# Linear attention with a rational FFN on one core: the hand-ordered instruction table is replaced by another one, and the last three slices share buffers

## The chip, the cores and the metric

One NeuronCore of a Trainium2 chip runs the whole program. The metric is device time in microseconds (us) of one execution. Five engines work from queues of their own: TensorE (PE, with its weight loads shown as PEld), VectorE (DVE), ScalarE (ACT), GpSimd (POOL) and SyncE (SP), which here issues the DMAs. An engine runs its queue strictly in order, and an instruction that needs another engine's result waits at the head of its queue.

## The reference

The inputs are r, k, v (4 batches, 8 heads, 768 steps, 48 wide), the decay w and the bonus u per head and channel, the two FFN weights w_in (384 x 2048) and w_out (2048 x 384), and the coefficients a (4) and b (2). The first stage is a recurrence over time:

```python
for t in range(S):
    cur = einsum('bhd,bhe->bhde', u * k[t], v[t])
    y[t] = einsum('bhd,bhde->bhe', r[t], state + cur)
    state = w * state + einsum('bhd,bhe->bhde', k[t], v[t])
```

Its output, as 3072 rows of 384, goes through an FFN whose activation is a ratio of a cubic and a quadratic:

```python
h = x @ w_in
P = a[0] + a[1]*h + a[2]*h**2 + a[3]*h**3
Q = 1 + |b[0]|*|h| + |b[1]|*h**2
out = (P / (Q + 1e-6)) @ w_out
```

## The kernel before, in words

**Attention.** Time is cut into 24 blocks of 128 rows (6 in each of 4 batches; block n is batch n % 4). For each block r and k are loaded (`Lr`, `Lk`) and multiplied with tables of powers of w (`sr`, `sk`), transposed on PE (`tr`, `tk`) and copied out of PSUM by ACT (`tre`, `tke`); PE makes the scores (`a`), DVE masks them (`ae`), PE makes the state's update (`kv`), which `kve` adds to the state, `ca` carries the state to the next block, PE makes the output (`y`). The bonus term is four multiplications and a sum on the side (`ba`, `bb`, `bs`, `bv`), and `ye` adds it. `x` transposes the block's output, and `xh`, `xl` split it into a high and a low part.

**FFN.** Two blocks make a tile of 256 rows (12 tiles). The 2048 hidden columns of a tile are 16 pieces j of 128; four of them make a slice (`SL`, line 36), and the last four pieces of the last tile are three slices of 2, 1 and 1: slices 47, 48 and 49 of 0 to 49. A slice s goes: `f1` on PE, nine matmuls per piece, into one of two PSUM buffers (h0, h1); three stages on ACT (`z`, `q`, and `t`), `u3` on DVE, `ln` and `ex` on ACT, then `hi`, `p`, `d`, `lo` on DVE; `f2` on PE, twelve matmuls for each of two halves; after a tile's last slice `os` takes the result out of PSUM and `od` stores it. `f1` of slice s+2 needs the buffer of slice s, so it waits for `lo` of slice s.

**Weights.** The 28 weight pieces come as 8-byte floats and are turned into pairs of 4-byte parts: `cl` loads one, ACT (`c0`, `cu`, `ch`), DVE (`c2`, `c3`) and POOL (`cr`, `co`) convert it.

**Which DVE work has all its inputs in SBUF.** The multiplications `sr`, `sk`, `ba`, `bb`, `bv` (lines 500 to 522), `ca` (line 611), the copy `LV` on DVE, `co` on DVE, and of the slice work only `p` (line 700, `q = (q + QE) * hi`). The other DVE work reads at least one operand from PSUM.

**Order.** Nothing here is scheduled by the compiler. `ORDER` (line 49) is a string of some 1,800 tasks, written by a search outside this file. A task is a name with its numbers, a letter for its engine (P, D, A, G for POOL, S for SP) and, where it takes a buffer, the buffer's name: `p.12D`, `hi.12Dta3`, `f1.12.0Ph0`. The program runs through the string once and issues each task to its engine, so the string fixes every engine's queue, which engine does a movable task, and which buffer is reused when. `warm.N` puts N small bf16 matmuls (line 797) without use into PE's queue, ahead of a task that follows them in the queue.

**End.** Line 371 and lines 374 and 375 (`flagt`, `flagm`) reduce a check on the inputs to one number, which all engines read at the end to skip a general path for odd inputs.

Of the kernel before, what the change touches and what calls it, by code (L numbers as in the profile page):

```python
# [49 lines left out]
pad.1G coefS plG mskG st0.0G st0.1G idG pad.0G wS Lv.3S betaA uwS ubG warm.54P ubpPpa0 cl_D ctrA st0.2A st0.3A Lv.2S LV.1.1.0A  # L50
LV.1.0.0A Lr.1S sqD Lr.2S pad.2G pow.0D pow.1D warm.10P turn.0.0Ppa1 warm.6P turn.1.0P inv.0D Lr.0S ubeA warm.13P turn.0.1Ppa0
pow.2D LV.1.0.1A Lk.0S Lk.2S warm.4P turn.2.0P tab.0A sr.1G inv.1D inv.2D warm.29P turn.2.1P Lk.1S Lv.0S LV.1.1.1A wlD turn.1.1P
tab.1A cl.2S tr.1Ph0 tre.1.0A tre.1.1A sr.0D wpPpa1 w128A cl.5S sr.2D sk.0D sk.2D ba.2Dm0 tr.0Ppa0 tre.0.1A warm.9P kv.2Ph1 sk.1D
tre.0.0A kve.2.0A bb.2D ba.0Dm1 Lr.3S ba.1Gm2 bs.2D bv.2D Lv.1S tk.0Ph0 tke.0A c0.2A c2.2Dh0 bb.1G kv.0Ppa1 kve.0.1A warm.2P
a.0Ppa0 bb.0G kve.2.1A warm.6P tk.1Ph1 c3.2D cu.2A cr.2Gta0 Lk.3S cl.6S tke.1A warm.16P a.1Ph0 kve.0.0A tk.2Ppa1 ae.0.1D cl.12S
bs.0D c0.5A ch.2A ae.0.0D bv.0G bs.1D LV.0.1.1A cl.1S ae.1.0D Lr.4S c2.5Dh1 LV.0.0.1A LV.0.0.0A ae.1.1D warm.36P kv.1Ph0 cl.4S
sr.3G c3.5D LV.0.1.0A y.0Ppa0 sk.3G ba.3Dm3 co.2D c0.6A bb.3D Lk.5S ca.0.1G cu.6A Lk.4S kve.1.0A c2.6Dh1 tke.2A ye.0D ca.0.0G
kve.1.1A c3.6D cr.6Gta1 c0.12A c2.12Dh0 c3.12D bv.1D warm.7P tr.2Ppa1 warm.2P kv.3Ppa0 c0.1A c2.1Dh1 c3.1D tre.2.0A cu.12A
cr.12Gta2 tre.2.1A bs.3D warm.13P x.0Ph0 cl.26S kve.3.0A kve.3.1A cu.5A warm.11P a.2Ppa1 ae.2.0D sr.4G y.1Ph1 tr.3Ppa0 ch.12A
cl.0S cu.1A sk.5G ae.2.1D ca.1.1G c0.4A warm.5P y.2Ppa1 ye.1D tk.3Ph1 xh.0A sk.4D tre.3.1A ca.1.0D xl.0D warm.3P tr.4Ph0 c0.26A  # L60
Lr.5S tre.3.0A tke.3A cr.5Gta3 ye.2D ba.4Dm1 c0.0A ch.6A warm.2P x.2Ppa0 xh.2A bv.3G c2.26Dh1 c3.26D cu.4A cr.1Gta4 xl.2D a.3Ppa1
warm.2P tk.4Ph1 ae.3.1D tre.4.0A sr.5G cl.20S Lv.5S tre.4.1A warm.21P kv.5Ph0 bb.4G cl.3S cl.9S ch.5A co.5G ae.3.0D c2.0Dpa0 c3.0D
ch.1A co.1G Lv.4S cu.20A tke.4A bs.4D c0.20A cl.10S cu.3A cl.11S kve.5.1D cu.0A cr.0Gta5 c2.4Dpa1 c3.4D cr.4Gta6 warm.16P x.1Ph1
xh.1A c0.3A xl.1D a.4Ppa0 warm.20P kv.4Ph1 cu.9A c2.3Dpa1 c3.3D cl.15S ch.0A co.0G cr.3Gta0 cu.26A cr.26Gta3 cl.14S cl.8S kve.5.0D
kve.4.1D c0.10A c2.10Dh0 c3.10D kve.4.0D warm.3P tk.5Ppa1 tke.5A cu.10A warm.14P y.3Ppa1 ye.3D c0.11A cu.11A ch.3A ba.5Gm0 c0.15A
f1.0.0Ph0 bv.4G LV.2.0.0S c2.11Dpa1 c3.11D cr.11Gta4 cu.15A LV.2.1.1S x.3Ph1 xh.3A ch.26A c0.9A c2.15Dpa1 c0.14A f1.0.1P f1.0.2P
bb.5G co.26G LV.2.1.0S ch.11A xl.3D tr.5Ph1 tre.5.1A tre.5.0A c3.15D co.12G ae.4.1D LV.2.0.1S ae.4.0D Lr.6S c2.14Dpa1 bs.5D
f1.0.3P warm.6P f1.1.0Ph1 cl.24S Lr.7S c3.14D z.0Ata5 c2.20Dpa0 c3.20D t.0Ata3 u3.0D warm.7P a.5Ppa1 ch.4A cu.8A cl.27S warm.1P
y.4Ppa0 cl.7S cl.13S ae.5.0D q.0A ln.0A f1.1.1P co.6G bv.5G cr.15Gta2 ch.15A ye.4D warm.5P x.4Ppa0 xh.4A cr.20Gta1 ch.20A Lk.6S
# [867 lines left out]
```

## Time and profile before

| | us |
|---|---|
| median of 3 runs | 567.09 (566.33 to 570.70) |
| the profiled execution, its own time | 566.86 |
| its span, first to last instruction | 565.1 |
| PE busy | 550.0 |
| DVE busy | 471.7 |
| ACT busy | 397.0 |
| POOL busy | 163.1 |

The span is what the traces count from; the profiled execution's own time is 1.8 us longer, and lies 0.2 us under the median. The mean granted TensorE clock is 0.997 of full speed. A "busy" PE is not PE at its peak: the ends of matmuls are modelled, and one that is 0.28 us long starts every 0.12 us.

### The profile page before, as it was taken

The page shows a single profiled execution, that of the slowest core. Times are in us where ns is not written, and L with a number is a line of the kernel's source. Part 1 is how long each engine was busy: PE and PEld are TensorE (multiplying, and loading weights), DVE is VectorE, ACT ScalarE, POOL GpSimd, SP SyncE. Part 2 cuts the span into 40 slices and gives each one's busy share as a digit, 9 for nine tenths or more (in the row PEclk, how much of TensorE's full clock was granted, in tenths as well). Part 3 has the DMA queues.
Part 4 walks back from the last instruction along what each step waited for, and adds up shares of the span by engine and source line. Part 5 has one row for each costly group of instructions (what it writes and reads, how often), then busy time and mean ns, then how long its engine had stood idle before and what let it go on. Part 6 is the DMA issues. An engine that isn't in the chain of part 4 may idle for free.

```text
span 565.1 us, 13792 instructions
## 1 busy us (share of the span) xinstructions
PE 550.0 (97%) x5916; PEld 527.3 (93%) x5916; DVE 471.7 (83%) x576; ACT 397.0 (70%) x522; POOL 163.1 (29%) x189
## 2 busy tenths in 40 slices
...
DMA packets 95273, 34.69 MB, mean 61 GB/s; under 512 B 88546, under 2 KB 91620, under 8 KB 95204
## 3 DMA queue, kind: packets, MB, share of 16 engines
...
## 4 chain that ended last, share of the span: by engine, by line
PE 71%; DVE 17%; ACT 6%; issue 3%; POOL 1%; DVEq 0%; ACTq 0%; POOLq 0%
PE h L644 26%; PE o L648 8%; PE o L650 8%; PE o L649 8%; PE y L600 4%; DVE q L700 4%; PE a L550 4%; DVE g L696 4%; PE kv L572 4%; DVE h L704 3%; PE idle_bank L797 3%; DVE h L691 3%; ACT z L683 2%; ACT z L687 2%; PE tk L527 2%
## 5 line engine op out<-in xcount | busy, mean ns | idle before, releaser
L644 PE MATMUL h<-xthi,wi 128*128 128x256 f32 x1152 | 218.3, 284 | 2.4 <-DVE l L709 2.1
L644 PEld LDWEIGHTS h<-xthi,wi 128*128 128x128 f32 x1152 | 180.6, 188 | 6.7 <-PE o L650 2.2
L644 PE MATMUL h<-xtlo,wi 128*128 128x256 f32 x576 | 160.8, 279 | 0.0
L648 PE MATMUL o<-wo,g 128*128 128x384 f32 x384 | 132.4, 345 | 0.0
L650 PE MATMUL o<-wo,l 128*128 128x384 f32 x384 | 129.5, 337 | 1.0 <-DVE l L709 1.0
L649 PE MATMUL o<-wo,g 128*128 128x384 f32 x384 | 129.2, 336 | 0.0
L644 PEld LDWEIGHTS h<-xtlo,wi 128*128 128x128 f32 x576 | 108.4, 188 | 0.0
L696 DVE SCALAR_TENSOR_TENSOR g<-h,sig,z 128x1024 fp32r<-128x1024 f32 (+2 forms) x50 | 61.9, 1238 | 47.1 <-ACT z L687 46.4
L679 ACT ACTIVATE z<-h,off,root 128x1024 f32<-128x1024 f32 (+2 forms) x50 | 58.6, 1172 | 42.6 <-PE h L644 34.2
L683 ACT ACTIVATE z<-q,sig 128x1024 f32<-128x1024 f32 (+2 forms) x50 | 56.0, 1119 | 30.6 <-DVE h L691 29.5
L670 ACT ACTIVATE q<-h 128x1024 f32<-128x1024 f32 (+2 forms) x50 | 49.5, 990 | 38.8 <-PE h L644 27.0
L650 PEld LDWEIGHTS o<-wo,l 128*128 128x128 f32 x384 | 72.2, 188 | 1.5 <-DVE l L709 1.5
L648 PEld LDWEIGHTS o<-wo,g 128*128 128x128 f32 x384 | 72.2, 188 | 0.8 <-ACT os L756 0.2
L649 PEld LDWEIGHTS o<-wo,g 128*128 128x128 f32 x384 | 72.3, 188 | 0.0
L691 DVE SCALAR_TENSOR_TENSOR h<-z,sig,h 128x1024 f32<-128x1024 f32 (+2 forms) x50 | 62.0, 1240 | 5.5 <-ACT z L679 3.0
L700 DVE SCALAR_TENSOR_TENSOR q<-q,sig,g 128x1024 f32<-128x1024 f32 (+2 forms) x50 | 64.6, 1292 | 1.9
L704 DVE SCALAR_TENSOR_TENSOR h<-h,sig,q 128x1024 f32<-128x1024 f32 (+2 forms) x50 | 62.5, 1250 | 1.6
L709 DVE TENSOR_TENSOR l<-h,z 128x1024 fp32r<-128x1024 f32 (+2 forms) x50 | 59.1, 1181 | 2.8 <-DVE h L704 0.5
L674 ACT ACTIVATE q<-q,off,root 128x1024 f32<-128x1024 f32 (+2 forms) x50 | 60.6, 1211 | 1.1
L687 ACT ACTIVATE z<-z 128x1024 f32<-128x1024 f32 (+2 forms) x50 | 51.4, 1027 | 1.5
L522 POOL TENSOR_TENSOR m<-vn,dt 128x384 f32<-128x384 f32 x16 | 15.3, 962 | 121.9 <-DVE dt L518 121.9
L508 POOL TENSOR_TENSOR m<-rh,kh 128x384 f32<-128x384 f32 x17 | 17.4, 1028 | 101.0 <-DVE rh L504 48.1
...
## 6 DMA issues: line engine op xcount, KB each, us to landing
...
coef<-in_moe_a_dram SPq DMA_DIRECT2D x1, 2.0 KB, 2.6
```

The lines of the kernel that those rows point to most:

```text
L644: nc.tensor.matmul(o, wi_of(j, cc, part), x_[:, cc], start=(n == 0), stop=(n == 3 * NCC - 1))
L648: nc.tensor.matmul(o, hi, wo_of(j, HI), start=first, stop=False)
L649: nc.tensor.matmul(o, hi, wo_of(j, LO), start=False, stop=False)
L650: nc.tensor.matmul(o, lo, wo_of(j, HI), start=False, stop=last)
L674: nc.scalar.activation(g["q"], g["q"], AF.Square, scale=RB, bias=KB)
L683: nc.scalar.activation(g["z"], g["q"], AF.Ln, bias=QE)
L687: nc.scalar.activation(g["z"], g["z"], AF.Exp, scale=-1.0)
L691: nc.vector.scalar_tensor_tensor(g["h"], g["t"], KAP, g["h"], op0=ALU.add, op1=ALU.mult)
L696: nc.vector.scalar_tensor_tensor(g["hi"], g["h"], c0, g["z"], op0=ALU.add, op1=ALU.mult)
L700: nc.vector.scalar_tensor_tensor(g["q"], g["q"], qe, g["hi"].bitcast(F32), op0=ALU.add, op1=ALU.mult)
L704: nc.vector.scalar_tensor_tensor(g["h"], g["h"], c0, g["q"], op0=ALU.add, op1=ALU.subtract)
L709: nc.vector.tensor_mul(g["lo"], g["h"], g["z"])
```

## The change

The whole of `ORDER` is replaced by another table of the same tasks. The new one comes from a search whose durations for GpSimd and DVE were read from the trace, and whose model lets GpSimd and DVE instructions run at the same time without ever excluding each other. What it moves is read off the two tables:

| | before | after |
|---|---|---|
| matmuls in `warm` groups, all / ahead of `f1.0.0` | 439 / 304 | 380 / 256 |
| DVE tasks with all inputs in SBUF, without the 50 `p` | 53 | 34 |
| of these ahead of `f1.8.0` in the table | 17 | 9 |
| POOL's elementwise tasks, all / ahead of `f1.8.0` | 166 / 95 | 190 / 101 |
| POOL tasks between `hi.s` and `lo.s` in the table, s = 0 to 8 | 13 | 32 |
| the same, s = 9 to 24 / s = 25 to 49 | 12 / 3 | 12 / 2 |
| `cl.6` in SP's queue | after `Lk.3` | after `Lr.0`, ahead of `Lr.2` |

The last tile's end is ordered anew, the last three slices share buffers, and a store may be issued by another engine than SP:

```diff
+f1.46.1P hi.45Dta0 p.45D d.45D flagmD f1.46.2P f1.46.3P z.46Ata2 f2.44.0P t.46Ata5 u3.46D q.46A ln.46A f2.44.1P lo.45Dta4
+f1.47.0Ph1 f1.47.1P ex.46A f2.45.0P f2.45.1P hi.46Dta1 p.46D d.46D lo.46Dta3 f1.48.0Ph0 f1.49.0P z.47Ata6 t.47A u3.47D q.47A
+ln.47A ex.47A hi.47Dta0 z.48Ata4 z.49A t.48A p.47D t.49A u3.48D d.47D u3.49D q.48A lo.47D q.49A ln.48A ex.48A hi.48Dta2 p.48D
+ln.49A ex.49A hi.49D d.48D p.49D lo.48D d.49D lo.49D f2.46.0P f2.46.1P f2.47.0P f2.47.1P f2.48.0P f2.48.1P f2.49.0P f2.49.1P
+os.49.0A od.11.0A os.49.1D od.11.1S
...
     def f1(s, jj):
         f, j0, _ = SL[s]
-        if jj == 0:
+        if s == NS - 1:
+            hps[s] = hps[s - 1][:, GW // 2 : GW]
+        elif jj == 0:
             hps[s] = ps_h.tile([P, GW], F32, tag=here[0], name=f"h{s}")
...
+    packs = {}
+    PACK = {NS - 3: (0, 0), NS - 2: (1, 0), NS - 1: (1, 2 * N1)}
+
     def ew_tile(s, nm, dt=F32):
         n = SL[s][2] * N1 if s in range(NS) else GW
+        if s in PACK:
+            place, at_ = PACK[s]
+            key = place, dt
+            if key not in packs:
+                packs[key] = ew.tile([P, GW], dt, tag=here[0], name=f"{nm}{s}")
+            return packs[key][:, at_ + n * (nm in "zl") : at_ + n * (nm in "zl") + n]
...
-    def put_dma(f, hf):
+    def put_dma(f, hf, e):
         bi, i = blk(2 * f + hf)
-        nc.sync.dma_start(out[ds(bi * S + i * P, P), :], oss.pop((f, hf)))
+        e.dma_start(out[ds(bi * S + i * P, P), :], oss.pop((f, hf)))
```

The order of the old table at the same place was `f1.47.0 f1.47.1 f2.45.0 ... f2.45.1 f1.48.0 f2.46.0 f2.46.1 f1.49.0 flagt flagm f2.47 f2.48 f2.49 os.49.0A od.11.0S os.49.1A od.11.1S`, with each of the last three slices in buffers of its own.

## Rows read from the trace of the kernel before

**Rows 1.** The page, section 1: busy us (share of the span) xinstructions.

```profile
PE 550.0 (97%) x5916; PEld 527.3 (93%) x5916; DVE 471.7 (83%) x576; ACT 397.0 (70%) x522; POOL 163.1 (29%) x189
```

**Rows 2.** Windows by stage, and `f1.45`, then `f2.43`: length, busy us (xinstructions), clock, DMA share, GB/s.

```profile
core 0: us, PE busy (x) PEld busy (x) DVE busy (x) ACT busy (x) POOL busy (x), PEclk, DMA share, GB/s
0.00:47.57 47.57, 44.30 (x866) 40.08 (x866) 40.92 (x88) 41.01 (x90) 32.36 (x51) 1.00 0.96 233
47.57:133.58 86.01, 83.95 (x932) 80.84 (x928) 81.77 (x101) 76.34 (x110) 65.87 (x66) 1.00 0.44 107
...
180.13:530.28 350.15, 348.42 (x3428) 337.03 (x3427) 283.77 (x308) 231.32 (x259) 44.97 (x51) 1.00 0.13 30
...
521.92:526.12 4.20, 4.20 (x38) 4.20 (x38) 1.83 (x2) 2.64 (x3) 0.00 (x0) 1.00 0.00 0
526.12:530.28 4.16, 4.16 (x26) 4.07 (x25) 3.98 (x5) 2.60 (x3) 0.00 (x0) 1.00 0.00 0
...
530.28:565.10 34.82, 26.83 (x170) 24.89 (x169) 20.76 (x27) 18.92 (x27) 0.00 (x0) 0.95 0.09 32
```

**Rows 3.** Waits of PE: who waited for whom, us in total, times, longest.

```profile
PE h L644 <- DVE l L709: 2.1, 4, 1.0
PE x L619 <- DVE m L605: 1.2, 1, 1.2
```

**Rows 4.** Timeline of PE around warm groups: start, length, instruction, [idle before].

```profile
29.65 0.78 PE L797 MATMUL idle_bank<-wones 128*128 128x128 bf16 x11
30.39 0.27 PE L550 MATMUL a<-ysa,kt 64*64 64x64 f32 x1
...
77.72 1.44 PE L797 MATMUL o<-wones 128*128 128x128 bf16 x23 [1.15 <-ACT os L756]
```

**Rows 5.** Timeline of ACT in the prologue: the first power table leaves PSUM.

```profile
10.41 0.48 ACT L348 COPY wrn<-ptab 128x384 f32<-128x384 f32 x1 [0.28 <-PE ptab L345]
```

**Rows 6.** Timelines of POOL and DVE around 62 us.

```profile
61.37 1.02 POOL L504 TENSOR_TENSOR rh<-rh,wrn 128x384 f32<-128x384 f32 x1
62.35 2.97 POOL L420 TENSOR_TENSOR wo<-bwo,wo 128x384 fp32r<-128x384 f32 x2
...
62.28 2.18 DVE L700 SCALAR_TENSOR_TENSOR q<-q,sig,g 128x1024 f32<-128x1024 f32 x1
```

**Rows 7.** Line 700, stretch 0 to 133.58 us: duration ns min/median/max.

```profile
L700 DVE SCALAR_TENSOR_TENSOR q<-q,sig,g x7: 1277/1285/2177, 62.3 to 128.2; 128x1024 f32<-128x1024 f32 x7
```

**Rows 8.** Groups by line: busy us, mean ns; line 700 to 133.58 us, line 500 whole.

```profile
L700 DVE SCALAR_TENSOR_TENSOR q<-q,sig,g 128x1024 f32<-128x1024 f32 x7 | 10.7, 1527 | 0.3
...
L500 DVE TENSOR_TENSOR kh<-kh,wkn 128x384 f32<-128x384 f32 x10 | 6.1, 622 | 0.8 <-DMA kh<-in_k_dram 0.8
```

**Rows 9.** Timelines of DVE, PE and ACT in the last tile, by time.

```profile
538.77 1.22 DVE L709 TENSOR_TENSOR l<-h,z 128x1024 fp32r<-128x1024 f32 x1
540.13 0.36 PE L644 MATMUL h<-xthi,wi 128*128 128x256 f32 x1 [0.98 <-DVE l L709]
545.20 1.23 DVE L709 TENSOR_TENSOR l<-h,z 128x1024 fp32r<-128x1024 f32 x1
548.55 0.75 DVE L696 SCALAR_TENSOR_TENSOR g<-h,sig,z 128x512 fp32r<-128x512 f32 x1 [1.46 <-ACT z L687]
556.60 0.48 DVE L700 SCALAR_TENSOR_TENSOR q<-q,sig,g 128x256 f32<-128x256 f32 x1
557.65 0.42 DVE L709 TENSOR_TENSOR l<-h,z 128x256 fp32r<-128x256 f32 x1
557.99 0.27 DVE L374 TENSOR_REDUCE oks<-flagt 1x1 f32<-1x128 f32 x1
558.29 0.14 DVE L375 CAST okf<-oks 1x1 int32<-1x1 f32 x1
558.61 1.11 ACT L756 ACTIVATE os<-o,sig 128x384 f32<-128x384 f32 x2 [2.63 <-PE o L650]
```

**Rows 10.** Timeline of SP at the end: both last stores.

```profile
559.22 1.66 SPq L764 DMA_DIRECT2D out_dram<-os  x2
```

More of the change, by code (lines that the diff above doesn't have):

```diff
@@ L49 @@
 ORDER = """
[L50 to L69, printed above, removed]
@@ new lines @@
+turn.2.0P tab.0A sr.0G cu.6A sr.2G warm.26P turn.0.1Ppa0 turn.2.1P inv.1D warm.8P turn.1.1P Lk.0S LV.1.1.1A c2.6Dh0 wlD ubeA
+tr.0Ppa1 tab.1A c3.6D Lk.1S tre.0.1A warm.8P wpPpa0 tre.0.0A sr.1G warm.2P tr.1Ph1 tre.1.0A tre.1.1A cl.2S Lv.0S sk.2D ba.2Dm0
+bb.2D bs.2D sk.0G warm.12P tk.0Ph0 ba.0Gm1 bb.0G kv.2Ppa1 cl.5S sk.1D bv.2D tke.0A a.0Ph1 ba.1Gm2 c0.2A kve.2.1A w128A kve.2.0A
+Lr.3S ae.0.0D c2.2Dpa0 Lv.1S cu.2A pad.2G ae.0.1D bb.1G warm.3P kv.0Ph0 Lk.3S kve.0.1A cr.6Gta0 cl.12S tk.1Ppa1 tke.1A bs.0D bv.0G
@@ new lines @@
+co.18G ae.8.0D u3.7D ae.8.1D f1.8.1P f1.8.2P f1.8.3P os.5.0D sr.9G LV.4.0.0S xh.6A xl.6D ln.7A ex.7A os.5.1D f2.6.0P x.7Ppa1
+ch.27A cu.25A cr.25Gta6 ch.25A c2.24Dpa0 c3.24D Lk.10S hi.7Dta3 p.7D tr.9Ppa0 tre.9.1A f2.6.1P ca.6.0G xh.7A ca.7.0G co.25G d.7D
+tre.9.0A xl.7D kv.8Ppa0 Lk.11S z.8Ata0 lo.7Dta1 kv.9Ppa1 kve.9.0D kve.9.1D cr.24Gta6 ch.24A t.8Ata2 u3.8D f1.9.0Ph1 f1.9.1P
+kve.8.0D sk.10G ba.10Gm2 bb.10G q.8A ln.8A ex.8A co.27D tk.9Ppa1 tke.9A ba.9Gm0 f1.9.2P f1.9.3P z.9Ata5 kve.8.1D bs.8D co.24G
@@ new lines @@
+bv.11G tke.11A x.10Ppa1 xh.10A tr.12Ppa0 Lr.15S f2.10.1P LV.6.1.1S tre.12.1A d.11D lo.11Dta5 bb.13D tre.12.0A a.11Ppa0 ae.11.1D
+ae.11.0D tk.12Ph1 Lk.15S Lk.14S sk.14G t.12Ata3 LV.6.0.1D sk.15G z.12Ata4 Lv.15S od.0.1S f2.11.0P LV.6.0.0D u3.12D Lr.14S
+kv.13Ppa0 kve.13.0D LV.6.1.0S tke.12A y.11Ph1 ye.11D kve.13.1D xl.10D os.11.0D f2.11.1P bs.13D ca.10.0G q.12A ln.12A ex.12A
+a.12Ppa0 tr.13Ppa1 tre.13.0A f1.13.0Ph1 hi.12Dta6 f1.13.1P ae.12.0D p.12D d.12D tre.13.1A tk.13Ppa1 tke.13A sr.15G lo.12Dta2
```

197 lines of the change are left out of this document (100 added, 97 removed).

## The prediction, made before the result was known

> **What bounds the kernel now.** I read the page first: PE is busy 550.0 us of 565.1, nothing else is near it [rows 1]. So a change of order can only win what PE doesn't need: stretches in which its queue holds filler, waits, and the tail. The split by stage says where these are [rows 2]. From 180 to 530 us PE is busy 348.4 of 350.2 us, while DVE has 66 us free, ACT 119, POOL 305: here PE alone sets the pace, and both tables give it the same matmuls. To 47.57 us, where the first `f1` starts, and on to 133.58 us, where `f1.8.0` starts, it is different: DVE is busy 81.8 of 86.0 us in the second stretch, ACT 76.3, POOL 65.9, and in the first all of them share the time with DMA (share 0.96). PE's busy figure hides there that it runs fillers. In the waits of PE almost nothing is left: 2.1 us in all on `lo` (four times) and one wait of 1.2 us [rows 3]. The timeline shows why: a filler group ends about when the data comes. Eleven fillers start at 29.65 us and the scores start at 30.39 [rows 4]. A filler costs (0.78 - 0.22) / 10 = 0.056 us, taking the length of one as 0.22, since starts are spaced more closely than lengths; so 439 of them are 24.6 us of PE's queue. In places they run longer than the wait that they fill: 23 of them follow at 77.72 a wait of 1.15 us that was there already [rows 4].
>
> The tail, from 530.28 us on, has PE busy 26.8 of 34.8 us [rows 2]: it waits 0.98 us for `lo.45` at 540.13, and ends at 559.1 us behind `lo.49`, which ends at 557.65 + 0.42 = 558.07 [rows 9].
>
> **Part 1, fewer fillers.** 439 - 380 = 59 fewer, 48 of them ahead of `f1.0.0`: 59 x 0.056 = 3.3 us off PE's queue. They are worth that only if the data that they waited for comes 3.3 us earlier. If it doesn't, a wait stands where the filler stood: what is late next is `lo` of the slice two back, and the blocks' chain `ye`, `xh`, `xl`. So the engines of the front decide.
>
> **Part 2, DVE's load in the front.** Ahead of `f1.8.0` eight SBUF-only tasks leave DVE (17 to 9), at 0.62 us, the mean of one kind of them with its collisions [rows 8]: -5.0 us of DVE. POOL gets six more elementwise tasks at about 1.02 us [rows 6]: +6 us on an engine that was busy 32.4 + 65.9 = 98.3 us of 133.6 [rows 2], so it has the room, though each result comes 1.02 - 0.62 = 0.4 us later than DVE would give it. By loads alone 3.3 us are there to be had.
>
> **Part 3, DVE against POOL.** At 62.28 us `p.0` takes 2.18 us, where the median is 1.285 [rows 6, 7]. A POOL `co` started at 62.35, one `co` takes 1.0 us, and the two in that row take 2.97 in place of 2.0 [rows 6]: `p` ran when the first `co` was done, and the second `co` when `p` was done. They take turns. The seven `p` to 133.58 us have a mean of 1.527 us [rows 8], so 7 x 0.242 = 1.7 us were lost on DVE. In the old table 13 POOL tasks stand between `hi.s` and `lo.s` for s = 0 to 8, and for four of the nine slices none at all; in the new table 32, with at least two in each slice. So nearly every `p` of the front now meets a POOL task. The trace shows no front in which all do, so I bound it: below by -1.7 (no `p` meets any; the table's order isn't the order of starts, and an engine that is late misses its partner), above by 9 x (2.18 - 1.285) = 8.1 us, that is 8.1 - 1.7 = +6.4 on DVE. I take half a POOL task per `p`, 9 x 0.5 - 1.7 = +2.8 us, since a blocked `p` meets the other task at any point of its 1.0 us. The 17 to 9 other tasks collide less than before; I leave that uncounted (under 1 us). After slice 8 the counts are the same in both tables (12 and 12, 3 and 2), so nothing is charged there, and a stretched `p` is covered by DVE's 66 free us.
>
> Sum of the front: DVE gives back 5.0 and loses 2.8, so its work gets 2.2 us shorter, while PE's queue is 3.3 us shorter. DVE was 95% busy in the second stretch, with 4.2 us free in gaps [rows 2], so I go by DVE and not by PE, and take off the 0.4 by which a result that POOL now makes comes later: **-1.8 us**. Bounds: -3.3 by PE, and by the upper bound of part 3 on DVE alone 6.4 - 5.0 = +1.4.
>
> Moves past SP's queue: `cl.6` (384 KB) now lands ahead of `Lr.2`, `Lr.1` and the `Lk`, which at the 233 GB/s of that stretch [rows 2] puts them 1.6 us back, and ACT has `c0.6` ahead of `tab.0`. Cover: nothing can be scaled before the first table is out at 10.41 + 0.48 us [rows 5], and the new table has POOL scale the first blocks one after the other at 1.02 us [rows 6]. If the cover is too short, it costs up to 1.6 us at the start; I take 0, and it is in the range.
>
> **Part 4, the tail.** Counted from `lo.45`, which ended at 538.77 + 1.22 = 539.99 us [rows 9]. The new table puts `flagm` ahead of `u3.46` on DVE: + 0.27 + 0.14 = 0.41, so `lo.45` ends about 540.5 and `f1.47` starts at 540.6 in place of 540.13: **+0.5**. After that `f1.48` and `f1.49` stand together ahead of `f2.46`, so `f2.46` covers slices 47 to 49. `f1.49` no longer waits for `lo.47`, because it has its own half of h0. PE's queue from 540.6 is `f1.47` (two pieces), `f2.45`, `f1.48` and `f1.49` (one each), `f2.46`, then half, a quarter and a quarter of an `f2`. A whole `f1` took 4.20 us and a whole `f2` 4.16 where PE ran without a wait [rows 2]: 4.20 + 3 x 4.16 = 16.7 us, and 0.2 for the last matmul to drain, 557.5. DVE and ACT against that: `lo.46` ended 546.43 - 539.99 = 6.44 us behind `lo.45` [rows 9]; the same distance puts it at 546.9, just when `f1.48` is due. Behind it DVE has 5 instructions of slice 47 at 0.75 and 10 of slices 48 and 49 at 0.48, 8.5 us, and once it must wait 1.46 us while ACT makes `ln` and `ex` of slice 47 [rows 9]; the other waits of that kind lie beside the work of a neighbouring slice. So `lo.49` ends near 556.9, where the third matmul of `f2.49` would want it at 556.6, and PE ends 0.3 us late, at 557.8 in place of 559.1: **-1.3 us**, the +0.5 included. The shared tiles add no instruction; a wait through them would show between `z.49` and slice 48, and I put 0 to +0.5 on it, taking 0.
>
> The last two evictions ran on ACT one after the other, 1.11 us [rows 9], and SP issued its second store until 559.22 + 1.66 = 560.88 [rows 10]. Now ACT and DVE take one each, and ACT issues one store: the second store's issue can end 0.7 us sooner after the last matmul. What lies behind it, landing and teardown, was 565.1 - 560.9 = 4.2 us, and engines other than SP take part in it; so 0 to -0.7, taken at **-0.4**.
>
> **Sum.** -1.8 - 1.3 - 0.4 = -3.5 us against the profiled execution: 566.86 - 3.5 = 563.4. The median of the runs lies 0.2 above that execution: **563.5 us**.
>
> **Rivals.** (a) *The front keeps to the new table.* `p` misses most of its partners, PE gains the full 3.3 us, and the 1.2 us wait on `ye` [rows 3] and the over-long fillers around 78 us don't come back: 3.3 + 1.7 + 1.2 to 2.5 gives 567.1 - 6.2 to 7.5 = 559.6 to 560.9. For it: all three engines' loads fall or have room. Against: 32 for 13. Chance 0.32. (b) *Only the tail wins.* Waits take the fillers' place one for one, 567.1 - 1.7 = 565.4. For it: fillers ended when the data came, so the data set the time. Chance 0.20. (c) *Slower: turns between DVE and POOL set the front.* Place: slices 0 to 8, where POOL prepares the blocks that PE waits for. Each `p` waits 0.89 us, and each POOL task behind a `p` 0.97 us [rows 6]; if a chain passes both engines, 9 x 0.89 - 1.7 + 9 x 0.97 - 5.0 = +10.0, and with the tail's -1.7 it is 575.4 us at worst; half of it on the path gives 570.4. It decides once the delays exceed the 4.2 us that DVE had free. The Trainium skill has this as a rule (SBUF — State Buffer, "SBUF: two separate sides"): a DVE instruction with two SBUF inputs and a GpSimd one that reads SBUF exclude each other, and the second "fully blocks". By that rule a table searched without exclusion is late wherever the two meet; the rows of `p.0` agree. Chance 0.10. (d) My forecast, 0.38.
>
> The change also trusts POOL's durations. In the rows the 1.02 us multiplication at 61.37 is followed by the next start 0.98 later [rows 6], so length and spacing agree. The Trainium skill speaks against it (Perfetto Trace Analysis, "GPSIMD Engine Instruction"): a GpSimd span is unreliable and should be timed by start-to-start spacing. By the row both give the same plan, and by the rule alone the sum would stay open by as much as part 2.
>
> **How the numbers follow.** About 1% (561.4 and 572.8) is what a measurement of this kernel can tell from no change. Faster than 561.4: nearly all of (a), 0.30, and 0.04 of (d): 0.34. Slower than 572.8: the worse half of (c), 0.05, and 0.02 for an unseen wait: 0.07. Within: 0.59. The range goes from the best end of (a), with the end's bound of -0.7 for -0.4 and some 0.3 for the earlier first filler (559.0), to just short of (c)'s half (569.5); left out are the rest of (a) and most of (c).
>
> **What would show it.** Right: fillers' count 380 with `f1.8.0` at 130 to 132 us; line 700 to that point at a mean near 1.8 us; `f1.49` directly behind `f1.48`, and PE's end 27.5 us after `f1.46.0` starts, in place of 28.8. Wrong: line 700 at 1.5 or below with PE early (a); waits of PE on `lo`, `ye` or `xh` of over 3 us in the front (b, c); POOL's `sk`, `sr`, `co` at means over 1.4 us (c); a wait of ACT or DVE between slices 48 and 49 (packing).

## The result

The new table takes 558.85 us (median of 4 runs, 558.10 to 559.88) against 566.97 us (median of 4): ratio 0.985, 95% interval 0.982 to 0.988. That is 8.1 us faster, where 3.5 were forecast, and 0.15 us below the low end of the range. The profiled execution took 558.4 us, its span is 556.7, and the granted clock 1.0.

By stage, with the same borders as [rows 2], which are the starts of `f1.0.0`, `f1.8.0` and `f1.46.0`, then the whole from `f1.8.0` to `f1.46.0` in the old kernel:

```profile
core 0: us, PE busy (x) PEld busy (x) DVE busy (x) ACT busy (x) POOL busy (x), PEclk, DMA share, GB/s
0.00:46.08 46.08, 42.39 (x818) 38.48 (x818) 38.90 (x80) 38.46 (x85) 38.13 (x58) 1.00 0.93 226
46.08:130.38 84.30, 82.49 (x917) 79.77 (x914) 80.53 (x100) 75.30 (x109) 67.67 (x68) 1.00 0.50 117
130.38:524.36 393.98, 393.47 (x3962) 382.33 (x3959) 324.31 (x359) 257.11 (x285) 79.84 (x91) 1.00 0.17 35
...
524.36:556.70 32.34, 25.89 (x170) 24.85 (x169) 20.32 (x28) 16.70 (x25) 0.00 (x0) 0.99 0.08 28
```
```profile
133.58:530.28 396.70, 394.96 (x3958) 381.45 (x3956) 328.23 (x362) 260.75 (x298) 64.90 (x74) 1.00 0.16 34
```

| stage | before | after | difference | forecast |
|---|---|---|---|---|
| to `f1.8.0` | 133.58 | 130.38 | -3.2 | -1.8 |
| `f1.8.0` to `f1.46.0` | 396.70 | 393.98 | -2.7 | 0 |
| `f1.46.0` to the end of the span | 34.82 | 32.34 | -2.5 | -1.7 |

The border at `f1.8.0` is fair: all fillers stand ahead of it, and without them PE has 866 + 932 - 439 = 1359 matmuls ahead of it in the old kernel and 818 + 917 - 380 = 1355 in the new one, four short ones apart.

The first stage is the least certain of these numbers, since the start of a program scatters (below). From `f1.0.0` to `f1.8.0` it is 84.30 us in each of the three kernels that share the new table up to there, and 86.01 to 86.03 in three with the old one, so 1.7 of the 3.2 us lie there and repeat. Ahead of `f1.0.0` the three new ones take 46.08 to 46.93 us and the three old ones 47.47 to 48.02.

The middle is the surprise. The 1.2 us of `x` on DVE [rows 3] are gone, and of these waits of PE in the new kernel only the last, on `xl`, lies in the middle:

```profile
PE o L808 <- DVE os L769: 1.2, 1, 1.2
PE h L644 <- DVE l L720: 1.1, 2, 0.9
PE kv L572 <- DVE xtlo L633: 0.3, 1, 0.3
```

What the wait view shows only in part is seen when the end of each `lo` is set beside the start of the `f1` that waits for it. In the old middle nine `f1` (10, 12, 21, 25, 33, 34, 35, 40, 46) start within 0.15 us of the end of their `lo`, in the new one two (9, 29). The old `f1.33`, as DVE and then PE show it: `lo.31` ends at 404.65, and PE starts 0.05 later. Such a start can be cheap: the matmul before it started at 404.43, and those ahead of that one follow each other at 0.17 us, so PE lost about 0.1 us here.

```profile
403.42 1.23 DVE L709 TENSOR_TENSOR l<-h,z 128x1024 fp32r<-128x1024 f32 x1
...
404.26 0.34 PE L649 MATMUL o<-wo,g 128*128 128x384 f32 x1
404.43 0.34 PE L650 MATMUL o<-wo,l 128*128 128x384 f32 x1
404.70 0.38 PE L644 MATMUL h<-xthi,wi 128*128 128x256 f32 x1
```

In the front, line 700 is now line 711. To `f1.8.0` its seven instructions, by time min/median/max and then by busy time and mean, answer to [rows 7, 8]; under them, one meeting with POOL in time order:

```profile
L711 DVE SCALAR_TENSOR_TENSOR q<-q,sig,g x7: 1275/1585/2224, 59.6 to 125.4; 128x1024 f32<-128x1024 f32 x7
```
```profile
L711 DVE SCALAR_TENSOR_TENSOR q<-q,sig,g 128x1024 f32<-128x1024 f32 x7 | 11.7, 1674 | 0.1
```
```profile
101.87 1.30 POOL L420 TENSOR_TENSOR wi<-bwi,wi 128x512 fp32r<-128x512 f32 x1 [0.73 <-ACT wi L417]
102.02 2.22 DVE L711 SCALAR_TENSOR_TENSOR q<-q,sig,g 128x1024 f32<-128x1024 f32 x1
103.12 2.97 POOL L508 TENSOR_TENSOR m<-rh,kh 128x384 f32<-128x384 f32 x2
```

`p.4` waits behind `co.23` until 103.17, and the next POOL task, 1.0 us long alone, waits behind `p.4`. `lo.4`, the third task after `p.4`, ends at 107.22, and `f1.6.0`, which needs it, starts at 107.28.

The tail, which answers to [rows 9, 10], DVE, PE, ACT and SP by time:

```profile
530.96 0.27 DVE L374 TENSOR_REDUCE oks<-flagt 1x1 f32<-1x128 f32 x1
531.26 0.14 DVE L375 CAST okf<-oks 1x1 int32<-1x1 f32 x1
531.34 1.29 DVE L702 SCALAR_TENSOR_TENSOR h<-z,sig,h 128x1024 f32<-128x1024 f32 x1
532.54 1.22 DVE L720 TENSOR_TENSOR l<-h,z 128x1024 fp32r<-128x1024 f32 x1
533.90 0.36 PE L644 MATMUL h<-xthi,wi 128*128 128x256 f32 x1 [0.90 <-DVE l L720]
539.03 1.23 DVE L720 TENSOR_TENSOR l<-h,z 128x1024 fp32r<-128x1024 f32 x1
550.66 0.58 ACT L767 ACTIVATE os<-o,sig 128x384 f32<-128x384 f32 x1 [3.70 <-PE o L650]
551.19 0.62 DVE L769 TENSOR_SCALAR os<-o,sig 128x384 f32<-128x384 f32 x1 [1.12 <-PE o L650]
551.28 0.38 ACTq L775 DMA_DIRECT2D out_dram<-os  x1
551.84 0.34 SPq L775 DMA_DIRECT2D out_dram<-os  x1
```

`f1.47` starts 9.54 us behind `f1.46` (before 9.85), `f1.49` runs directly behind `f1.48` (541.48 behind 540.32), and PE's last matmul ends 26.8 us behind `f1.46.0` (before 28.8). From the issue of the last store to the span's end it is 4.5 us (before 4.2).

### The profile page after: what moved, and what is told of

Its sections match the earlier page's. It is cut to its first block, busy times and chain, and to the rows that moved or that the text cites. A ratio compares the mean times of both kernels' runs of the same rounds, so it can differ in the third digit from the quotient of the medians.

```text
span 556.7 us, 13698 instructions
## 1 busy us (share of the span) xinstructions
PE 544.2 (98%) x5857; PEld 525.4 (94%) x5857; DVE 464.1 (83%) x564; ACT 387.6 (70%) x502; POOL 185.6 (33%) x215
## 4 chain that ended last, share of the span: by engine, by line
PE 64%; DVE 16%; ACT 8%; issue 3%; POOL 2%; DVEq 0%; ACTq 0%; POOLq 0%
PE h L644 26%; PE o L648 8%; PE o L650 8%; PE o L649 8%; DVE q L711 4%; PE y L600 4%; DVE g L707 3%; PE a L550 3%; DVE h L715 3%; DVE h L702 3%; ACT z L694 2%; ACT z L698 2%; PE kv L572 2%; PE tk L527 1%; DVE l L720 1%
## 5 line engine op out<-in xcount | busy, mean ns | idle before, releaser
L650 PE MATMUL o<-wo,l 128*128 128x384 f32 x376 | 126.5, 337 | 0.0
L707 DVE SCALAR_TENSOR_TENSOR g<-h,sig,z 128x1024 fp32r<-128x1024 f32 x47 | 60.3, 1283 | 45.3 <-ACT z L698 44.7
L690 ACT ACTIVATE z<-h,off,root 128x1024 f32<-128x1024 f32 x47 | 56.7, 1206 | 46.3 <-PE h L644 40.2
L694 ACT ACTIVATE z<-q,sig 128x1024 f32<-128x1024 f32 x47 | 54.1, 1152 | 22.6 <-DVE h L702 21.4
L711 DVE SCALAR_TENSOR_TENSOR q<-q,sig,g 128x1024 f32<-128x1024 f32 (+2 forms) x50 | 68.0, 1360 | 1.6
L702 DVE SCALAR_TENSOR_TENSOR h<-z,sig,h 128x1024 f32<-128x1024 f32 x47 | 60.3, 1284 | 7.1 <-ACT q L681 4.2
L720 DVE TENSOR_TENSOR l<-h,z 128x1024 fp32r<-128x1024 f32 x47 | 57.4, 1222 | 2.2
L698 ACT ACTIVATE z<-z 128x1024 f32<-128x1024 f32 x47 | 49.9, 1061 | 1.5
L500 POOL TENSOR_TENSOR kh<-kh,wkn 128x384 f32<-128x384 f32 x21 | 23.1, 1103 | 77.5 <-DMA kh<-in_k_dram 77.3
L508 POOL TENSOR_TENSOR m<-rh,kh 128x384 f32<-128x384 f32 x20 | 21.7, 1086 | 53.7 <-PE x L619 52.6
```

What stands on the lines that cost most here:

```text
L650: nc.tensor.matmul(o, lo, wo_of(j, HI), start=False, stop=last)
L694: nc.scalar.activation(g["z"], g["q"], AF.Ln, bias=QE)
L698: nc.scalar.activation(g["z"], g["z"], AF.Exp, scale=-1.0)
L702: nc.vector.scalar_tensor_tensor(g["h"], g["t"], KAP, g["h"], op0=ALU.add, op1=ALU.mult)
L707: nc.vector.scalar_tensor_tensor(g["hi"], g["h"], c0, g["z"], op0=ALU.add, op1=ALU.mult)
L711: nc.vector.scalar_tensor_tensor(g["q"], g["q"], qe, g["hi"].bitcast(F32), op0=ALU.add, op1=ALU.mult)
```

## The experiments

Every kernel was run beside the old one on the same chip; a ratio is to that. Times of single stages are from the one profiled execution of each, and the start of the program alone moves by up to 0.9 us between executions (`f1.0.0` at 46.08, 46.54 and 46.93 us in three kernels whose tables are the same up to slice 25: the new one, `new_mid_meet`, `new_mid_beside`). "Old" and "new" are the two tables. The new kernel's four runs are of another batch; where a time is set beside its 558.85 us, the two didn't run side by side.

### The tail alone

```diff
 (old table up to f1.46.0, then)
-f1.46.0P ... f1.49.0Ph1 ... od.11.1S
+the new tail, PACK, f1 of slice 49 in half of h0, od.11.0A
```

> The old table up to f1.46.0, then the new tail with its shared buffers and the store from ACT. Theory (the tail gives what the traces show): PE's end comes 2.0 us sooner behind f1.46.0 and the last stores 0.46 us sooner, so 566.97 - 2.5 = 564.5 us, f1.49 directly behind f1.48. The prediction's own terms (-1.3 and -0.4) would give 565.3. Rival (the new tail only pays because the new table delivers lo.45 and the stores earlier): no gain, 566.5 to 567.5.

564.54 us, ratio 0.997 [0.995, 0.999]. From `f1.46.0` to the span's end it takes 32.65 us against 34.82 [rows 2], so the tail's 2.2 us come without the rest of the new table. PE's last matmul ends 27.5 us behind `f1.46.0`, 1.3 sooner than before as the prediction had it, and not the 2.0 of the theory; `f1.47` starts 10.23 us behind it, 0.38 later than before. That the total came out as in the theory is luck.

### The middle: DVE relieved, and DVE loaded

First the old table with a lighter DVE:

```diff
-bb.10D bv.8D sk.12D sr.11D ... ca.12.1D ca.10.1D sk.15D ...   (33 tasks behind f1.8.0)
+bb.10G bv.8G sk.12G sr.11G ... ca.12.1G ca.10.1G sk.15G ...
```

> The old table with the 33 DVE tasks behind f1.8.0 that have all inputs in SBUF (sr, sk, ba, bb, bv, ca) given to POOL; nothing else. Theory (the middle was not PE alone: lo ended less than 0.15 us ahead of its f1 seven times, and x.11 waited 1.2 us on ye.13 behind ca.12.1, ca.10.1 and sk.15): the wait of x.11 goes and the small ones on lo shrink, -1.5 to -3.0 us, 564.0 to 565.5. Rival, the step of the prediction (from 180 to 530 us PE alone sets the pace): 0, 566.7 to 567.2. A second rival (POOL is slower by 0.4 us each and delays ye and the kv): up to +1.

564.58 us, ratio 0.995 [0.994, 0.997]. The wait of `x` on `ye` is gone from the list of PE's waits, and `f1.15.0` comes 1.3 us sooner. DVE and PE there, first in the old kernel, then in this one (`m` is written by `ye`):

```profile
211.95 1.49 DVE L611 TENSOR_TENSOR vs<-vs,w 48x192 f32<-48x192 f32 x2
213.47 1.27 DVE L500 TENSOR_TENSOR kh<-kh,wkn 128x384 f32<-128x384 f32 x1
...
219.88 0.55 DVE L605 TENSOR_TENSOR m<-y,m 128x384 f32<-128x384 f32 x1
220.49 0.55 PE L619 MATMUL x<-identw,m 128*128 128x128 f32 x3 [1.20 <-DVE m L605]
```
```profile
217.93 0.55 DVE L607 TENSOR_TENSOR m<-y,m 128x384 f32<-128x384 f32 x1
219.21 0.49 PE L621 MATMUL x<-identw,m 128*128 128x128 f32 x3
```

The window from `f1.12.0` to `f1.46.0`, which answers to 180.13 to 530.28 in [rows 2]:

```profile
180.30:528.90 348.60, 347.77 (x3429) 336.98 (x3427) 270.23 (x280) 231.15 (x259) 67.94 (x77) 1.00 0.13 30
```

DVE's busy time in it falls by 13.5 us and the stage by 1.55, though DVE had 66 us free there before. From `f1.8.0` to `f1.46.0` the gain is 1.85 us, and all but 0.08 of it lies ahead of `f1.25.0` (200.28 to 198.51 us). From there to `f1.46.0`, old kernel and this one:

```profile
333.86:530.28 196.42, 196.10 (x1664) 191.65 (x1665) 153.74 (x159) 130.75 (x140) 10.48 (x11) 1.00 0.08 20
332.56:528.90 196.34, 196.02 (x1666) 191.53 (x1665) 150.37 (x151) 130.91 (x140) 18.54 (x21) 1.00 0.08 20
```

Of the nine late `lo`, those of `f1` 10, 12, 21 and 25 are early now (0.36 us or more ahead); those of 33, 34, 35, 40 and 46 are as late as before, so this run's gain doesn't come from them.

Then the opposite, the new table with meetings added, and its control:

```diff
 ex.sA                    (s = 25 to 44)
+bes.sG bes.sG            (POOL: scr = z[:, 0:384] * wrn; the control has one)
```

> The new table with two multiplications of no use on POOL (128x384, SBUF to SBUF) behind each ex.s, s = 25 to 44, so that the second of them is under way when p.s starts. Every p of these 20 slices then should take about 2.1 us in place of 1.285, 16 us of DVE in all, in a stretch where DVE has over 40 us free. Theory (lo sets f1 in places of the middle: ten of the 20 f1 of the new table start less than 0.9 us behind their lo): PE waits on lo there for 2 to 4 us, 560.9 to 562.9. Rival, the step of the prediction (a stretched p of the middle is covered by DVE's free time): 558.5 to 559.3.

> The control for the meeting of p and POOL: the new table with one multiplication of no use on POOL behind each ex.s, s = 25 to 44, in place of two. It runs beside hi.s, which reads PSUM and SBUF, and is over before p.s starts. Theory (the 8 us came from p waiting, which took 1.80 us in place of 1.29 and came through to PE by the two h buffers): p at 1.29 again, 558.5 to 559.3 us. Rival (POOL's mere use of the slice's buffers holds things up): half of the loss or more, 563 or above.

567.65 us with two, ratio 1.000 [0.998, 1.002]; 559.98 with one, ratio 0.986 [0.983, 0.989]. The same PE work, `f1.25.0` to `f1.46.0`, first with two, then with one:

```profile
326.73:532.18 205.45, 200.10 (x1735) 194.43 (x1733) 165.87 (x160) 131.68 (x136) 58.90 (x53) 1.00 0.06 17
```
```profile
327.16:526.15 198.99, 198.19 (x1735) 194.57 (x1733) 157.62 (x160) 131.37 (x136) 34.24 (x33) 1.00 0.06 17
```

The 21 `p` of these windows took 1804 and 1379 ns in the mean. Of the 20 in the slices with the added work, 17 were stretched in the first kernel and 4 in the control, where they still met another POOL task. PE's waits on `lo` in the two, and one meeting of the first:

```profile
PE h L648 <- DVE l L724: 3.3, 5, 0.9
```
```profile
PE h L647 <- DVE l L723: 0.6, 1, 0.6
```
```profile
395.98 2.11 POOL L785 TENSOR_TENSOR scr<-z,wrn 128x384 f32<-128x384 f32 x2 [3.42 <-ACT z L702]
397.25 1.92 DVE L715 SCALAR_TENSOR_TENSOR q<-q,sig,g 128x1024 f32<-128x1024 f32 x1
398.05 2.01 POOL L517 TENSOR_TENSOR m<-m,ub 128x384 f32<-128x384 f32 x1
```

8.25 us more of DVE make the stage 6.46 us longer, while DVE is free for 198.99 - 157.62 = 41 us. I had expected 2 to 4. So the free time isn't slack. As I read it, it is DVE waiting for ACT inside the chain `f1`, ACT, `u3`, ACT, `hi`, `p`, `d`, `lo`, `f1` two slices on, and that chain is as long as PE's two slices: in the new kernel `f1.33.0` starts at 399.90, `lo.33` ends at 416.89, and PE, which has no wait between, is ready for `f1.35.0` at 417.20. The control uses the slice's buffers too and the same stage of it takes 0.9 us more than the new kernel's 198.10, so most of the loss is that of the stretched `p` and not of POOL's use of the buffers. That POOL's own tasks start later behind two multiplications than behind one isn't taken out by it; PE's list has 3.3 us on `lo`, 1.2 us of issue and 0.6 us on `xl`.

### The fillers

```diff
-old table, 439 fillers      +the same with 380 (each group cut in proportion)
-new table, 380 fillers      +the same with 439; and each table without any
```

> The old table with 380 fillers in place of 439, 256 of them ahead of f1.0.0, every group cut in proportion; nothing else. Theory A (the data set the front: a filler group of the old table ends 0.05 to 0.4 us behind its data, so a wait takes the filler's place): between -0.8 and 0 us, 566.2 to 567.0, with the waits of PE in the front up by 2.5 to 3.5 us. Theory B (PE's queue alone carries the front, a filler is pure cost): -3.3 us, 563.7.

> The new table with 439 fillers in place of 380, 304 of them ahead of f1.0.0, every group stretched in proportion; nothing else. Theory A and B both say that PE, whose groups end 0.05 to 1.2 us behind their data in the new table too, starts everything later by 59 x 0.056 = 3.3 us, less what the few real waits behind them absorb (1.2 us on os, at 71 us): 561.0 to 562.2. Rival (the fillers stand where PE has to wait anyway, by turns between DVE and POOL): 558.9 to 559.5.

> The old table without any filler. Theory (the data set the old front): f1.8.0 comes where it was, 132.5 to 133.6 us, as long as the granted clock stays at 1.0: 565.5 to 567.2. Rival (fillers in PE's queue cost what they take): f1.8.0 up to 24.6 us earlier less waits, some 125 us, 558. If the granted clock falls to half in stretches where PE now waits, the matmuls behind take twice as long: +2 to +10 us, and the profile's clock shows it.

> The new table without any filler. Theory (the new front is earlier because its data are earlier; groups end 0.05 to 1.2 us behind their data): f1.8.0 at 129.0 to 130.4 us against 132.5 to 133.6 for the old table without fillers, so the distance of about 3 us stays: 557.5 to 558.9. Rival (the new front is earlier because of its 59 fewer fillers): both tables without fillers bring f1.8.0 within 1 us of each other. A fallen clock costs either table +2 to +10 us.

The old table with 380: 567.20 us, ratio 1.000 [0.998, 1.002], theory A. Waits took the fillers' place: PE's listed waits to `f1.8.0` rise by 1.5 us, from 5.1 to 6.6, where I had expected 2.5 to 3.5, and `f1.8.0` comes 0.25 us sooner, which is lost again ahead of `f1.25.0`. The new one with 439: 560.20 us, ratio 0.990 [0.987, 0.993], 1.4 us more than 558.85 by the medians, between what the theories said. In the trace PE is 1.55 us later at the end, but 1.32 of that are there at `f1.0.0`, where the start's scatter is 0.9; so how much of the 3.3 us was absorbed by waits stays open.

Without fillers the new table takes 562.68 us, ratio 0.992 [0.989, 0.994]. The old one's ten times spread from 565.4 to 575.0 us; the four longest, from 573.8, have a mean granted clock of 0.975, the shortest has 0.995. Its ratio of 1.000 [0.996, 1.004] leaves out the three longest, and its profiled execution is the longest of all; so what fillers are worth to the old table as a whole stays open, and that trace is left aside.

In the new table without fillers PE ran slowly in three places. The first is the start: `f1.0.0` comes at 49.79 us in place of 46.08, more than the start's scatter. Four transposes took 1.08 us there and 0.63 in the new kernel:

```profile
14.30 1.08 PE L526 MATMUL tr<-identw,rh 128*128 128x128 f32 x4 [0.65 <-ACT ub L298]
```
```profile
13.32 0.63 PE L527 MATMUL tr<-identw,rh 128*128 128x128 f32 x4
```

Small matmuls of `kv` start every 0.08 us at 18.6 us and every 0.04 from 23.0 on, and the trace's entries for the clock begin at 22.96 us (in the new kernel at 6.80), so the 1.00 that the windows give for this stretch isn't a measured clock; by the spacing it was the lower level, 1.2 GHz. PE's first matmul that isn't a filler starts at 9.4 us here and at 9.3 in the new kernel, where fillers run ahead of it. The other two places are the stretch behind `f1.0.0` and the one around `f2.1`, each shown behind the stretch ahead of it:

```profile
46.00:49.79 3.79, 2.19 (x56) 1.83 (x50) 3.73 (x6) 3.79 (x9) 3.79 (x4) 1.00 1.17 286
49.79:55.80 6.01, 6.01 (x42) 6.01 (x39) 4.49 (x10) 3.63 (x8) 5.93 (x7) 0.72 1.05 192
76.00:80.00 4.00, 2.25 (x14) 1.93 (x13) 3.96 (x4) 3.98 (x7) 4.00 (x4) 1.00 0.31 124
80.00:84.00 4.00, 4.00 (x17) 3.82 (x16) 4.00 (x7) 3.83 (x5) 3.84 (x5) 0.62 0.00 0
```

PE was busy 2.19 of 3.79 us and 2.25 of 4.00, and behind that the clock was at 1.2 GHz for a good part of the stretch (0.72 and 0.62 in the mean). With fillers the new kernel has 1.00 in each stage of the table above but the last, which has 0.99. At `f1.8.0` the kernel without fillers is 5.15 us behind the new one, 3.7 of them from ahead of `f1.0.0`.

### The front: one cause at a time

Four reliefs of the old front, all with 380 fillers, so that no filler hides a gain:

```diff
-sr.0D sr.2D sk.0D ba.0D sk.4D ca.1.0D ba.4D sr.6D   +the same on G          (old_front_pool_380)
-c0.20A c0.15A ch.3A c0.10A cu.10A c2.10D c3.10D     +behind f1.0.0          (old_act_380)
-ba.3D bb.3D ca.1.0D ba.4D            +the same on G, with the edit of old_act_380 (old_act_dve_380)
-ch.15A ch.20A ... ex.0A                             +ex.0A ch.15A ch.20A    (old_slice0_380)
```

> The old table with 380 fillers, and eight of the DVE tasks ahead of f1.8.0 that have all inputs in SBUF (sr.0, sr.2, sk.0, ba.0, sk.4, ca.1.0, ba.4, sr.6) given to POOL, at their old places. With 380 fillers alone the old table gained nothing, so any gain here is that of DVE's load. Theory (DVE's load sets the front: eight tasks at 0.62 us are 5.0 us): f1.8.0 moves from 133.3 to 130 or 131 us, -2 to -3.3 us, 563.9 to 565.2. Rival (the order of all engines' queues, the loads and ACT's among them, makes the new front, and DVE's load is a small part; POOL's result comes 0.4 us later each): -0.7 to +1, f1.8.0 at 132.6 to 134.3.

> The old table with 380 fillers, in which conversions that no early f1 or f2 needs are put behind f1.0.0, as the new table has them: c0.20, c0.15, ch.3, c0.10 and cu.10 on ACT (about 3 us of it) and c2.10, c3.10 on DVE (1.2 us). Theory (ACT, busy 45.4 of 47.5 us from 20 to 67.5, sets the old front together with DVE, and the new table's gain there is work put off): f1.0.0 comes 1 to 1.5 us sooner (46.0 to 46.6), f1.2.0 0.5 to 2 us sooner, and 565.2 to 566.8 us. Rival (what is put off comes back ahead of f1.2.0, whose lo.0 waits in the same queues): f1.0.0 sooner, f1.2.0 and all behind as before, 566.8 to 567.6.

> The same, and ba.3, bb.3, ca.1.0 and ba.4 given from DVE to POOL (2.2 us of DVE ahead of f1.0.0). Theory (DVE and ACT set the front together, so only relief of both counts): sooner than the one before by 0.5 to 1.5 us, f1.2.0 at 65 to 66.5, 564.2 to 566. Rival (POOL, 15.8 of 17.6 us busy from 30 to 47.6, is full there as well and hands its results over later): the same as the one before or up to 1 us later.

> The old table with 380 fillers, and ACT's ch.15 and ch.20 behind ex.0 in place of ahead of it. In the old trace ln.0 ends at 58.30 and ex.0 starts at 59.80, with ch.15, xh.4 and ch.20 between; in the new one ex.0 follows ln.0 at once. Theory (the chain of slice 0, on which f1.2.0 waits, is what the front's fillers covered): lo.0 0.8 to 1.3 us sooner, f1.2.0 at 66.1 to 66.7 (xl.5 holds it at 65.8 at the earliest), 566.0 to 566.8 if that lasts. Rival (it comes back as a wait on the late conversions or on lo.1): 567.0 to 567.5.

Ratios 0.999, 1.001, 1.000, 1.000, with intervals that reach 0.002 to 0.003 to either side; `f1.8.0` at 134.05, 133.19, 134.17 and 133.83 us against 133.58. Each time the rival came true, as far as `f1.8.0` and the ratio tell (`old_slice0_380` took 567.94 us, 0.4 above its rival's range, beside 567.63 for the old kernel). In `old_front_pool_380` DVE was busy 120.2 us of the first 134, 2.5 us less than in the old kernel, and nothing came of it. The old kernel from 30 us to `f1.2.0` shows how close its engines lie:

```profile
30.00:47.57 17.57, 17.45 (x377) 15.76 (x374) 16.41 (x30) 17.05 (x35) 15.80 (x17) 1.00 1.02 311
47.57:67.50 19.93, 19.30 (x273) 18.48 (x270) 18.67 (x26) 19.35 (x31) 17.23 (x17) 1.00 1.02 291
```

ACT is busy 97% of the 37.5 us, DVE 94%, POOL 88%.

### The tables cut at `f1.3.0`

```diff
+new table to f1.3.0, then the old one            (hy_no3, 387 fillers)
+old table to f1.3.0, then the new one            (hy_on3, 432 fillers)
+hy_no3 with the 33 tasks on POOL                 (hy_no3_mid)
+hy_no3_mid with the new tail                     (hy_no3_mid_tail)
```

> The new table up to f1.3.0, then what is left of the old one in the old order, old tail included (buffers renamed where the seam needs it). In the traces the new table has f1.3.0 2.5 us sooner. Theory (the whole order of the first 80 us is worth its 2.5 us and what lies behind keeps the distance): 564.2 to 565.3, f1.8.0 at 130.5 to 131.5. Rival (the old order behind it waits for its own reasons and the gain is given back by f1.8.0): 566.5 to 567.3. The seam itself may cost up to 1 us.

> The reverse: the old table up to f1.3.0, then what is left of the new one, new tail included. Theory: the loss of the front's 2.5 us and nothing else, 561.0 to 562.2. Rival (front and rest are not separable; the new rest needs the state that the new front leaves): 563 or above.

> The new table up to f1.3.0, then the old one, with the old one's 33 SBUF-only DVE tasks behind f1.8.0 given to POOL; old tail. The kernel without that last part had f1.8.0 1.2 us sooner than the old table and gave 0.9 of it back behind it, in waits on lo. Theory (the old middle is paced by lo, so PE can't keep what the front gives it until DVE is relieved): the 1.2 us and the 2.7 us of old_mid_pool add up, 563.0 to 563.8 us, and f1.46.0 at 527.3 to 528.0. Rival (the two are the same microseconds): 564.3 to 565.0, as old_mid_pool alone.

> The same with the new tail, its shared buffers and the store from ACT. Theory (parts add up once lo doesn't pace): another 2.2 to 2.6 us, 560.6 to 561.5 us; what is then left to the new table, 1.7 to 2.6 us, is its order from 81 to 180 us and the small waits of the middle. Rival (tail and middle share): 562 or above.

`hy_no3`: 567.11 us, ratio 0.998 [0.996, 1.001]. The rival came: `f1.3.0` is 2.2 us sooner than in the old kernel, `f1.8.0` 1.2, `f1.46.0` 0.3. What is lost up to `f1.8.0` is lost between `f1.3.0` and `f1.4.0` (7.57 us, before 6.46), right behind the cut, and may be the cut's own. The other 0.9 us go in the old order behind `f1.8.0`:

```profile
0.00:81.35 81.35, 76.49 (x1200) 71.57 (x1200) 72.41 (x126) 71.97 (x134) 68.78 (x89) 1.00 0.93 230
81.35:132.34 50.99, 50.04 (x543) 47.81 (x542) 49.65 (x58) 42.00 (x58) 39.10 (x39) 1.00 0.18 33
132.34:529.97 397.63, 395.22 (x3958) 381.35 (x3956) 329.18 (x362) 260.40 (x298) 65.61 (x74) 1.00 0.16 34
```

The last stage is 0.9 us longer than the old kernel's 396.70 with the same instructions. `hy_on3`: 563.10 us, ratio 0.991 [0.988, 0.994], 4.3 us behind the new kernel: 2.7 at `f1.3.0`, 4.7 at `f1.8.0`, and 4.6 all the way to the end. So the new order behind `f1.8.0` keeps a distance, and the old one doesn't; at the seam, 2 us may be the cut's own.

`hy_no3_mid`: 564.41, ratio 0.996 [0.995, 0.997], the same as with the 33 tasks alone. In its one trace PE's last `f2` starts 1.3 us sooner than in `old_mid_pool` (555.36, 556.67), but the times don't show it; undecided. With the tail: 562.99, ratio 0.993 [0.991, 0.995], 1.4 us more, less than expected. All three parts stacked on the old order are worth 3.9 of the 8.1 us.

### Fewer fillers, and the check's end moved forward

```diff
-warm.38P kv.1 ... warm.7P y.5 ... warm.19P f1.4.0    (78 fillers less in eight places)
+warm.20P kv.1 ... y.5 ... warm.4P f1.4.0             (new_trim)
-flagt, flagm in the last tile                        +in slice 44, as well (new_trim_flag)
```

> The new table with 302 fillers in place of 380: 78 taken from the nine groups that ended 0.4 to 1.2 us behind their data (ahead of kv.1, y.5, x.5, tr.7, f1.2.0, tk.6, f2.1.0 and f1.4.0). Theory (there PE's queue is late, not the data): 0.5 to 2 us sooner, 557.0 to 558.4. Rival (the data behind each group depend on the PE work ahead of it and on full engines, so the next wait takes it up): 558.5 to 559.2. A third way (a wait instead of a filler lets the granted clock fall, as in the table without fillers): up to +1.

> The new table with 302 fillers, and flagt and flagm moved from the last tile's tail to slice 44, where DVE waits for ex.44 anyway. In the new trace flagm took 0.41 us of DVE right ahead of u3.46 and lo.45, for which f1.47.0 waited 0.9 us. Theory (the tail runs on DVE's chain): 0.4 us sooner than with 302 fillers alone, 557.2 to 557.8. Rival (f1.48 and lo.46 hold the tail): no difference, 557.8 to 558.2.

557.90 us, ratio 0.984 [0.981, 0.986], and 557.35, ratio 0.981 [0.978, 0.983]: 1.0 and 1.5 us below the new kernel's median, with intervals that overlap its 0.982 to 0.988. So by the times each step is at the edge of what these runs tell. The traces say more of the first: from `f1.0.0` to `f1.8.0` it is 83.07 and 83.08 us in these two, and 84.30 in the three kernels with 380. `f1.46.0` to `f1.47.0`, with the fillers cut and then with `flagm` moved too, shows the second:

```profile
523.67:533.20 9.53, 8.64 (x63) 8.32 (x62) 6.90 (x8) 7.55 (x8) 0.00 (x0) 1.00 0.11 42
```
```profile
523.68:532.81 9.13, 8.54 (x62) 8.25 (x61) 6.54 (x6) 7.55 (x9) 0.00 (x0) 1.00 0.11 43
```

The 0.40 us are about `flagm`'s 0.27 + 0.14, but not all of it is won: the matmul `flagt` moved across the border too, and `f1.44.0` to `f1.45.0` takes 0.12 us longer for it.

## Why the prediction was wrong

**The middle, charged nothing (-2.7).** The failed step is "here PE alone sets the pace, and both tables give it the same matmuls", and with it "a stretched `p` is covered by DVE's 66 free us". The matmuls were the same; the pace was not PE's alone. [rows 2] showed 348.4 of 350.2 us busy, and I read the missing 1.7 as nothing, though [rows 3] named 1.2 of it. What the runs show in its place is DVE's queue: `x` waited 1.2 us for a `ye` behind `ca` and `sk`, and the `lo` of four `f1` up to 25 were late. The new table has two of the three tasks ahead of that `ye` on POOL, and 25 tasks of that kind on DVE behind `f1.8.0` where the old one has 36. That PE alone doesn't set the pace is shown from both sides: relief of DVE in the old middle gives 1.85 us of this stage, load on it in the new one costs 6.5 us for 8.25. The relief took 33 tasks off DVE, where the new table takes 11 off and puts others elsewhere; whether these alone would bring the 1.85, and where the other 0.9 us of the 2.7 come from, isn't shown. It isn't the late `lo` of 33 to 46: summed over PE's matmuls (the time to the start of the next one, less the median for that pair of kinds), PE loses about the same from `f1.25.0` to `f1.46.0` in both kernels, within 0.1 us, and in the new one about 3 us less from `f1.8.0` to `f1.25.0`.

**The front, -1.8 against -3.2.** The size of part 1 (PE's queue 3.3 us shorter) came out by luck, for its reason did not hold: 59 fillers less in the old table gave nothing. I went by DVE: its busy time to `f1.8.0` fell from 122.7 to 119.4, 3.3 us, where I had 2.2, because part 3 was mis-sized: the seven `p` lost 11.7 - 7 x 1.285 = 2.7 us in place of 1.7, so +1.0 and not +2.8 (I had charged nine `p`, and only seven run ahead of `f1.8.0`); two of the seven missed POOL and three met only the end of a task. But DVE's load isn't the cause by itself either, since giving eight tasks to POOL in the old front changed nothing, nor are ACT's load, both together, or the order on ACT in slice 0. What the runs leave is the order of the first 80 us as a whole with the new order behind it (-2.2 at `f1.3.0` in `hy_no3`, and in `hy_on3`, without it, 2.7 behind the new kernel there). With ACT, DVE and POOL all near full ahead of `f1.2.0`, relief of one lets the next one hold; that is my reading, and which waits the new order undoes together stays open. Part 2's and part 3's meetings are real and the rival (c) has its mechanism: `f1.6.0` and `f1.9.0` start 0.06 us behind a `lo` that followed a stretched `p`. Between `f1.5.0` and `f1.10.0` PE loses 1.4 us more than in the old kernel (summed over its tasks: the time to the start of the next one, less the shortest for that kind), which fits that the exclusion, which the search leaves out, took back part of the gain; no run isolates it.

The Trainium skill's rule that I cited (SBUF — State Buffer, "SBUF: two separate sides": the second of the two "fully blocks") agrees with all of these rows, in both directions: 2.22 us for `p` behind `co.23`, and 2.01 for a POOL multiplication of 1.0 behind `p`.

**The tail, -1.3 against -2.0 at PE.** `f1.48` and `f1.49` together, no wait between slices 48 and 49, and PE's end 0.3 us behind what its queue alone would take came as forecast. The mis-sized term is the +0.5 for `flagm`: `f1.47` came 0.3 us sooner behind `f1.46`. In `tail_new`, with the old table ahead of it, the forecast holds: `f1.47` comes 0.38 later and PE's end 1.3 sooner. So the part was right for the tail alone, and what it lacked is that the new order ahead of the tail brings `lo.45` earlier by more than `flagm` costs. **The end, -0.4:** the second store's issue ends 1.71 us behind the start of PE's last `f2`, before 2.47, so 0.8 sooner where I had 0.7. From there to the span's end it is 4.5 us and before 4.2, which is within the scatter of the end (below), so the -0.5 of these two executions agrees with the forecast by luck.

**Moves past SP's queue, 0:** nothing in the runs speaks against it, but the start's own scatter of 0.9 us hides as much.

Rival (a) came nearest (559.6 to 560.9). It had the full 3.3 us and the wait on `ye`, but also the 1.15 us at 77.72 [rows 4], which did not go: its counterpart is the 1.2 us on `os` in the list of waits. It lacked the rest of the middle and 0.8 us of the tail, and its condition, that `p` misses most of its partners, did not hold: five of seven were stretched. So it is near in part by luck. I gave it 0.32, and set against it a count of partners (32 for 13) whose price on PE was at most near 1.4 us. Two of my signs of being right came without the forecast being right: `f1.8.0` at 130.38 us, within 130 to 132, and `f1.49` directly behind `f1.48`. Neither looks at the middle.
